# RWKV6 attention and an exact-GELU MLP on one core: six more zero products in the first tile

## The chip, the cores and the metric

The kernel runs on one core of a Trainium2 chip. The time is device microseconds of one execution; a kernel is timed several times and the median is given. An execution with the hardware profiler leaves the trace from which the times inside the kernel are read. They count from the start of the span, the time from the first instruction to the last.

## The reference

`r`, `k`, `v`, `w` have the shape (4, 8, 768, 48): 4 sequences, 8 heads, 768 steps, 48 channels. A linear attention with a decaying state runs over the steps, and its output goes through an MLP of 384 to 2048 to 384 with an exact GELU.

```python
for t in range(S):
    cur = np.einsum('bhd,bhe->bhde', u[None] * kt, vt)
    y[:, :, t] = np.einsum('bhd,bhde->bhe', rt, state + cur)
    state = wt[:, :, :, None] * state + np.einsum('bhd,bhe->bhde', kt, vt)
...
x = y.transpose(0, 2, 1, 3).reshape(B * S, H * D)
h = x @ w_in
g = 0.5 * h * (1.0 + erf(h * inv_sqrt2))
out = g @ w_out
```

## The kernel before, in words

**Tiles.** The 3072 tokens are cut into eight tiles of T = 384 steps, two for each sequence. `attention(x, unit)` is a Python generator that issues the attention of tile x, one step per `next()`; `mlp(x)` does the same for the MLP. While tile x's MLP runs, tile x + 1's attention is woven into it. The first tile has no MLP to be woven into. Its attention is cut into two units of four heads each, unit 0 and unit 1 (`units_of(0)` is 2, and 1 for every other tile), and these are woven into each other.

**The order by hand.** The scheduler is off. `PLAN[0]` is a string of letters that says which generator issues next: `.` is unit 0, `s` is unit 1, `l` is loads of weights and of tile 1's data, `c` is the conversion of weights, `f` is the attention of tile 1. Each engine executes its instructions in the order in which they were issued, and waits on semaphores for what it needs from the others. Unit 1 starts behind unit 0 and overtakes it at h = 16.

**Inside a unit.** Steps are taken in chunks of C = 64. For each unit there are NI = 6 pairs of chunks, and for each level h in 1, 2, 4, 8, 16, 32 three steps:

- `products` (L478 to L491): 24 products of 64 x 64 on TensorE, four for each of the six pairs of chunks (`g` and `p` each run over two halves of the partitions). An f32 product is executed as two passes, each with its own weight load (LDWEIGHTS) and product (MATMUL), so a call makes 48 pairs of instructions at line L485. For the levels from 2 to 16 it ends with `keep_warm(2)`, and the diagonal products of h = 1 do too.
- an update of `r` and `k` on VectorE (L563; L552 where they are updated one by one). It writes what the products have read, so it waits for them.
- a copy of the result out of PSUM into `a_sb`, with a mask on VectorE (L581) for h below 16, and by rows on ScalarE (L578) for h = 16. At h = 32 the copies are at L778.

After the levels, `k` is transposed on TensorE (L754, six products) and copied to SBUF on ScalarE (L767). Then come `kv` (L804: 24 products in f32, again 48 pairs of instructions), the products of the chunk matrices with `v` (L857), the chain over the states on VectorE (L836, L831), a copy of two columns as a fence (L867 or L870), the products of `r` with the states (L900), and the copy of the result into `xT` (L907, L923). In kv each index `i` of the six is four products of two passes, 8 pairs of instructions.

On TensorE, with u0 and u1 for the units, the order from the middle of the first tile on is: u0 h = 8, u1 h = 8, u1 h = 16, u0 h = 16, u1 h = 32, u1's transposes, u0 h = 32, u1's kv, u0's transposes, u1's L857, u0's kv, u1's L900, u0's L857, u0's L900. Then the first products of tile 1 (L501) and the first tile's MLP (L1299) follow.

**Zero products.** `keep_warm(n)` takes a bank of PSUM from the two with the tag "mm" and issues n products of a 128 x 128 matrix of zeros with 512 columns of zeros in bf16, each with its weight load. Nothing reads the result. Before the first products there is a `keep_warm(16)`. The tag "mm" is also used by the transposes of the first tile (`kt_ps`), by unit 0's `y_ps`, and by the MLP's banks.

**Instructions.** Each engine's instructions are read from memory by DMA while the kernel runs. In the trace, such transfers are of the kind "instruction", on queues 8 and 14.

Of the kernel before, what the change touches and what calls it, by code (L numbers as in the profile page):

```python
# [21 lines left out]
C = 64  # L22
# [6 lines left out]
NI = Q * N3  # L29
LEVELS = (1, 2, 4, 8, 16, 32)  # L30
# [46 lines left out]
def kernel(  # L77
# [47 lines left out]
    def pair(name):  # L125
        return pools["d"].tile([128, 2, BANK], F32, name=name, tag="d")
# [25 lines left out]
    def units_of(x):  # L152
        return NPART if x == 0 else 1
# [90 lines left out]
    def keep_warm(n):  # L244
        t = ps.tile([128, BANK], F32, name="warm", tag="mm", bufs=2)
        for _ in range(n):
            nc.tensor.matmul(t, lhsT=zeros[:, 0:128], rhs=zeros, start=True, stop=True)
# [42 lines left out]
    for i, h in enumerate(QUARTERS[:1]):  # L290
        for a in range(3):
            w_q = (3 - a) * C // 4
            z = q_ints[1 if a == 0 else 2]
# [82 lines left out]
    def attention(x, unit):  # L376
# [3 lines left out]
        np_ = len(parts)  # L380
# [6 lines left out]
        rc, kc = (z.rearrange("p (b i c t) -> p b i c t", b=np_, c=2, t=C) for z in (r, k))  # L387
# [87 lines left out]
        else:  # L475
            yield

        def products(bs, right, width, rest=False, last=False):  # L478
            d = pair("d")
            n = 0  # L480
            for b in bs:
                for i in range(NI):
                    for g in range(2):
                        for p in range(2):
                            nc.tensor.matmul(d[half[p], g, n * width:(n + 1) * width],  # L485
                                             lhsT=kc[half[g], b, i, p], rhs=right(half[g], b, i, p),
                                             start=True, stop=True)
                    n += 1
            if x == 0 and not rest and not last:
                keep_warm(2)  # L490
            return d[:, :, 0:n * width]  # L491

        def first_and_diagonal():

            width, each = 3 * C // 2, np_ * NI // 3
            for z in range(3):
                d = pair("d")
                for n in range(z * each, (z + 1) * each):
                    for g in range(2):
                        for p in range(2):  # L500
                            nc.tensor.matmul(d[half[p], g, (n - z * each) * width:(n - z * each + 1) * width],  # L501
                                             lhsT=kc[half[g], n // NI, n % NI, p], rhs=wide_r[half[g], 2 * n + p],
                                             start=True, stop=True)
                first_parts.append((at[:, :, z * each:(z + 1) * each],
                                    d[:, :, 0:each * width].rearrange("p g (n t) -> p g n t", t=width)))

        def copy_first_and_diagonal():
            for a, d in first_parts:
                a2 = a.rearrange("p g n (m two) -> p g n m two", two=2)[:, :, :, :, 1]
                for o, mask, data in ((a2, masks[1], d[:, :, :, 0:C // 2]), (a, masks[0], d[:, :, :, C // 2:])):  # L510
                    nc.vector.copy_predicated(out=o, mask=mask.unsqueeze(1).unsqueeze(1).to_broadcast(data.shape), data=data)
# [3 lines left out]
        def diagonal():  # L515
            return [products([b], lambda z, b, i, p: rucs[b][z, i, p], C) for b in range(np_)]

        def copy_diagonal(diag):
            for b in range(np_):
                nc.vector.copy_predicated(out=at[:, :, b * NI:(b + 1) * NI],  # L520
                                          mask=masks[0].unsqueeze(1).unsqueeze(1).to_broadcast([128, 2, NI, C]),
                                          data=diag[b].rearrange("p g (i t) -> p g i t", t=C))

        def halves():

            for h in LEVELS:
                m = C // 2 // h
                if x and h == 1:
                    first_and_diagonal()
                elif np_ < NPART:  # L530

                    d = products(range(np_), lambda z, b, i, p: rc[z, b, i, p], C, h == 1, h == LEVELS[-1])
                    d = d.rearrange("p g (n m two j) -> p g n m two j", two=2, j=h, m=m)[:, :, :, :, 1, :]
                else:
                    right = rc.rearrange("p b i c (m two j) -> p b i c m two j", two=2, j=h)[:, :, :, :, :, 1, :]
                    d = products(range(np_), lambda z, b, i, p: right[z, b, i, p], C // 2)
                    d = d.rearrange("p g (n m j) -> p g n m j", j=h, m=m)
                if h == 1:
                    yield
                    if x == 0:  # L540
                        diag = diagonal()
                yield

                r2 = r.rearrange("p (n two j) -> p n two j", two=2, j=h)[:, :, 1, :]
                t2 = tot[h].rearrange("p (n two) -> p n two", two=2)[:, :, 0:1].to_broadcast(r2.shape)
                k2 = k.rearrange("p (n two j) -> p n two j", two=2, j=h)[:, :, 0, :]
                tk = tot[h].rearrange("p (n two) -> p n two", two=2)[:, :, 1:2].to_broadcast(k2.shape)
                rk = bass.AP(tensor=r2.tensor, offset=r2.offset, ap=[r2.ap[0], [n_u - h, 2]] + list(r2.ap[1:]))
                tt = bass.AP(tensor=t2.tensor, offset=t2.offset, ap=[t2.ap[0], [1, 2]] + list(t2.ap[1:]))

                def update(z, r2=r2, t2=t2, k2=k2, tk=tk):
                    nc.vector.tensor_mul(*((k2, k2, tk) if z is k else (r2, r2, t2)))  # L552

                if x == 0 and m == 1:

                    update(k)
                    last_r.append(lambda: update(r))
                elif x == 0 and h == 1:
                    update(r)
                    yield  # L560
                    update(k)
                else:
                    nc.vector.tensor_mul(rk, rk, tt)  # L563
                yield
                if first_parts and h == 1:
                    copy_first_and_diagonal()
                    yield
                    continue
                ah = at.rearrange("p g n (m two j) -> p g n m two j", two=2, j=h)[:, :, :, :, 1, :]
                if x == 0 and m == 1:  # L570
                    last_rows.append((ah, d))
                    return
                if h >= 16:

                    for p in range(2):
                        for i in range(m):
                            s = slice(p * 64 + i * 2 * h, p * 64 + i * 2 * h + h)
                            nc.scalar.copy(out=ah[s, :, :, i], in_=d[s, :, :, i])  # L578
                else:
                    mask = masks[h].rearrange("p (m j) -> p m j", j=h).unsqueeze(1).unsqueeze(1)  # L580
                    nc.vector.copy_predicated(out=ah, mask=mask.to_broadcast(ah.shape), data=d)  # L581
                if h == 1:
                    copy_diagonal(diag)
                yield
# [154 lines left out]

        last_r, last_rows = [], []  # L740
        yield from halves() if x < 2 else quarters()


        if x < 2:
# [38 lines left out]
            def k_t(b, i, p, g):  # L783
                return kts[b][half[p], i, g, :]
# [9 lines left out]
        def vs(b, i, g):  # L794
            o = ((parts[b] * NI + i) * 2 + g) * D
            return loaded[x][1][:, o:o + G]

        kvs = []
        for b in range(np_):
            kv_ps = pair("kv_ps")  # L800
            for i in range(NI):
                for p in range(2):
                    for g in range(2):
                        nc.tensor.matmul(kv_ps[half[g], p, i * D:(i + 1) * D], lhsT=k_t(b, i, p, g),  # L804
                                         rhs=vs(b, i, g)[half[p], 0:D], start=True, stop=True)
            kvs.append(kv_ps[:, :, 0:NI * D].rearrange("p c (q i e) -> p q i c e", q=Q, e=D))
            if x > 0:
                o = parts[b] * Q * NC * D
                nc.scalar.copy(out=st[:, o:o + Q * NC * D].rearrange("p (i c e) -> p i c e", c=2, e=D),
                               in_=kv_ps[:, :, 0:NI * D].rearrange("p c (i e) -> p i c e", e=D))  # L810
# [628 lines left out]


    units = [attention(0, unit) for unit in range(units_of(0))]
    second = load_second(nc.sync)

# [104 lines left out]
```

## Time and profile before

| | us |
|---|---|
| median of 3 runs | 584.7 |
| lowest, highest | 584.18, 585.9 |
| the profiled execution | 587.26 |
| its span | 585.5 |
| TensorE busy in the first 6.17 us | 3.88 |
| TensorE busy from 6.17 to 46.18 us (40.01) | 29.83 |
| TensorE busy from 46.18 to 110 us (63.82) | 63.82 |
| TensorE's mean granted clock from 6.17 to 46.18 us | 0.91 |

The page gives for each engine the time in which at least one of its instructions was executing. PE is TensorE's products, PEld its weight loads, DVE is VectorE, ACT is ScalarE, and SP the engine that issues most of the DMAs. A view of instructions in order of time merges neighbours of one line and operation: start, length from the first start to the last end, how many (x), and in square brackets how long the engine sat idle before, and what ended that. "issue" means that the trace shows nothing that the engine waited for. Lengths of products hold a tail of about 0.2 us in which the result drains, and products that follow overlap it. Of each `keep_warm(2)` the trace has both weight loads and one of the two products. PEclk is the share of full speed that the clock gate granted to TensorE.

### The profile page before, as it was taken

How to read it: one execution, taken by the hardware profiler on the slowest of the kernel's cores; microseconds unless marked ns; L12 is line 12 of the kernel's file. 1: busy time of each engine (PE TensorE's matmuls, PEld its weight loads, DVE VectorE, ACT ScalarE, POOL GpSimd, SP SyncE). 2: the span in 40 equal slices, each digit the busy share in tenths (PEclk: the TensorE clock that was granted, in tenths of full speed). 3: DMA queues.
4: the chain of work that ended last, by engine and by line, in shares of the span. 5: the costliest groups of instructions: out<-in, count | busy, mean ns of one | idle time of the engine just before them, and what ended most of it. 6: DMA issues, size and time to landing. Idle time of an engine off the chain costs nothing. (4 is left out here: it accounts for less than half of the span.)

```text
span 585.5 us, 17244 instructions
## 1 busy us (share of the span) xinstructions
PE 569.1 (97%) x7407; PEld 507.7 (87%) x7418; DVE 460.2 (79%) x820; ACT 299.4 (51%) x735; POOL 8.0 (1%) x21
## 2 busy tenths in 40 slices
PE   7679999999999999999999999999999999999998
PEld 4466666766799999999999999999999999999997
DVE  7779877999768996698859998498759999884532
ACT  2565999432623556545554366455564366533400
POOL 4100000000000000000000000000000000000000
PEclk9989999999999999999999999999999999999999
DMA  7548771140222201441024201441013200210000
GB/s 248 188 154 295 253 260 55 34 142 3 41 75 78 75 3 31 124 135 57 2 55 122 74 21 19 115 139 38 2 32 116 68 2 1 43 40 7 1 15 34
DMA packets 51003, 46.79 MB, mean 80 GB/s; under 512 B 31728, under 2 KB 36080, under 8 KB 50928
## 3 DMA queue, kind: packets, MB, share of 16 engines
q1 hardware_dynamic: 50832, 45.62, 25.9%
q8 instruction: 58, 0.95, 0.7%
q14 instruction: 17, 0.14, 0.1%
q10 hardware_dynamic: 96, 0.07, 0.1%
HBM read 36.24 MB, written 4.72 MB: 70 GB/s over the span
## 5 line engine op out<-in xcount | busy, mean ns | idle before, releaser
L1087 PE MATMUL h_ps<-xT,w_in_sb 128*128 128x192 f32 x408 | 81.7, 331 | 0.4 <-DVE u L1429 0.3
L1087 PEld LDWEIGHTS h_ps<-xT,w_in_sb 128*128 128x128 f32 x408 | 67.6, 190 | 3.8 <-ACT g L1119 1.1
L1299 PE MATMUL h_ps<-xT,w_in_sb 128*128 128x384 f32 x192 | 64.2, 491 | 0.1
L1299 PEld LDWEIGHTS h_ps<-xT,w_in_sb 128*128 128x128 f32 x192 | 35.8, 190 | 23.9 <-ACT rkw L1407 0.2
L1313 PE MATMUL o_ps<-w_out_sb,g 128*128 128x192 f32 x224 | 39.5, 326 | 0.0
L1313 PEld LDWEIGHTS o_ps<-w_out_sb,g 128*128 128x128 f32 x224 | 36.9, 190 | 0.3
L669 ACT COPY a_sb<-d 32x256 f32<-32x256 f32 (+8 forms) x90 | 32.6, 362 | 3.3 <-PE d L653 1.4
L1313 PE MATMUL o_ps<-t,s 128*128 128x192 f32 x176 | 30.9, 328 | 0.0
L1313 PE MATMUL o_ps<-w_out_sb,f 128*128 128x192 f32 x176 | 30.9, 328 | 0.0
L1313 PE MATMUL o_ps<-t,g 128*128 128x192 f32 x176 | 30.8, 329 | 0.0
L1313 PE MATMUL o_ps<-t,e 128*128 128x192 f32 x176 | 30.7, 328 | 0.0
L1313 PE MATMUL o_ps<-w_out_sb,e 128*128 128x192 f32 x176 | 30.7, 328 | 0.0
L485 PEld LDWEIGHTS d<-rkw 64*64 64x64 f32 x1056 | 18.3, 140 | 13.6 <-issue 8.1
L1087 PE MATMUL u_ps<-s,w_in_sb 128*128 128x192 f32 x160 | 29.5, 328 | 0.0
L1313 PEld LDWEIGHTS o_ps<-t,s 128*128 128x128 f32 x176 | 28.8, 190 | 0.3 <-DVE u L1421 0.2
L1313 PEld LDWEIGHTS o_ps<-t,g 128*128 128x128 f32 x176 | 28.7, 190 | 0.3
L1313 PEld LDWEIGHTS o_ps<-w_out_sb,e 128*128 128x128 f32 x176 | 28.7, 190 | 0.2
L1313 PEld LDWEIGHTS o_ps<-w_out_sb,f 128*128 128x128 f32 x176 | 28.8, 190 | 0.2
L1313 PEld LDWEIGHTS o_ps<-t,e 128*128 128x128 f32 x176 | 28.7, 190 | 0.2
L1302 ACT ACTIVATE g<-h_ps 128x256 f32<-128x256 f32 (+1 forms) x32 | 13.8, 430 | 28.5 <-PE h_ps L1299 28.5
L485 PE MATMUL d<-rkw 64*64 64x64 f32 (+1 forms) x1056 | 20.9, 228 | 6.6 <-issue 4.2
L653 PE MATMUL d<-kx,rkw 64*64 64x96 f32 x1056 | 27.1, 247 | 0.0
(248 smaller groups left out, 1202.8 us busy)
## 6 DMA issues: line engine op xcount, KB each, us to landing
rkw<-in_rkw_dram SPq DMA_DIRECT2D x54, 256.0 KB, 3.6
raw<-in_w_out_dram SPq DMA_DIRECT2D x8, 768.0 KB, 4.8
v_in<-in_v_dram SPq DMA_DIRECT2D x8, 584.0 KB, 4.5
raw<-in_w_in_dram SPq DMA_DIRECT2D x5, 768.0 KB, 6.9
out_dram<-o_sb SPq DMA_DIRECT2D x20, 192.0 KB, 1.9
rkw<-kx SPq DMA_DIRECT2D x72, 48.0 KB, 2.0
rkw<-in_rkw_dram SPq DMA_DIRECT2D x6, 384.0 KB, 4.7
raw<-in_w_in_dram SPq DMA_DIRECT2D x9, 256.0 KB, 5.1
```

The source lines that it names most:

```text
L485: nc.tensor.matmul(d[half[p], g, n * width:(n + 1) * width], lhsT=kc[half[g], b, i, p], rhs=right(half[g], b, i, p), start=True, stop=True)
L653: nc.tensor.matmul(o[half[p], i * 3 * C // 2:(i + 1) * 3 * C // 2], lhsT=kc[half[g], n // NI, n % NI, p], rhs=rx[half[g], 2 * n + p], star ...
L669: nc.scalar.copy(out=at[z, g, first:behind, (a + 1) * h:], in_=d[z, :, :, to] if g == slice(None) else d[z, :, to])
L1087: nc.tensor.matmul(o, lhsT=lhsT, rhs=rhs, start=start, stop=True, skip_group_check=True)
L1299: nc.tensor.matmul(h_ps, lhsT=w_in_sb[:, f // FI, j, f % FI * 128:(f % FI + 1) * 128], rhs=xT[:, j, :], start=(j == 0), stop=(j == NJ - 1))
L1302: nc.scalar.activation(out=gs[group][:, f % FG, 0:t], in_=h_ps[:, 0:t], func=AF.Gelu)
L1313: nc.tensor.matmul(o, lhsT=lhs(j), rhs=rhs(j), start=start and j == 0, stop=(j == HF - 1), skip_group_check=True)
```

## The change

`products` gets an argument `hold`: after the `hold`-th pair of chunks, three zero products are issued inside the burst. It is set in one place, to 1, for unit 1 at h = 8. In kv, three zero products are issued after the fifth of the six indices, for unit 0 of the first tile alone. Nothing else differs.

```diff
-        def products(bs, right, width, rest=False, last=False):
+        def products(bs, right, width, rest=False, last=False, hold=None):
             d = pair("d")
             n = 0
             for b in bs:
...
                     n += 1
+                    if n == hold:
+                        keep_warm(3)
             if x == 0 and not rest and not last:
                 keep_warm(2)
...
-                    d = products(range(np_), lambda z, b, i, p: rc[z, b, i, p], C, h == 1, h == LEVELS[-1])
+                    d = products(range(np_), lambda z, b, i, p: rc[z, b, i, p], C, h == 1, h == LEVELS[-1], 1 if unit and h == 8 else None)
...
                         nc.tensor.matmul(kv_ps[half[g], p, i * D:(i + 1) * D], lhsT=k_t(b, i, p, g),
                                          rhs=vs(b, i, g)[half[p], 0:D], start=True, stop=True)
+                if units_of(x) > 1 and not unit and i == NI - 2:
+                    keep_warm(3)
             kvs.append(kv_ps[:, :, 0:NI * D].rearrange("p c (q i e) -> p q i c e", q=Q, e=D))
```

## The prediction

> **What bounds the kernel now.** I read the page first, then the engines' busy time in stretches of 3.41 us, then TensorE's instructions in order of time, then the DMA queues around its two longest waits.
>
> ```profile
> PE 569.1 (97%) x7407; PEld 507.7 (87%) x7418; DVE 460.2 (79%) x820; ACT 299.4 (51%) x735; POOL 8.0 (1%) x21
> ...
> q8 instruction: 58, 0.95, 0.7%
> ```
>
> TensorE is busy for 97% of the span, and the waits that the trace names for it lie almost all before 46 us. From there to the end its busy time has only about 1 us of holes, outside the last few microseconds. So what the first tile gains or loses by 44 us should reach the end nearly undiminished. Queue 8 carries 58 transfers of 0.95 MB, 16.4 KB each: instructions being fetched.
>
> ```profile
> core 0: us, PE busy (x) PEld busy (x) DVE busy (x) ACT busy (x) POOL busy (x), PEclk, DMA share, GB/s
> ...
> 16.41:19.82 3.41, 2.12 (x66) 1.35 (x68) 3.41 (x7) 3.38 (x6) 0.47 (x1) 1.00 0.81 210
> ...
> 23.24:26.65 3.41, 1.06 (x34) 0.71 (x35) 0.69 (x1) 0.62 (x1) 0.00 (x0) 1.00 0.35 114
> 26.65:30.06 3.41, 2.73 (x73) 2.14 (x78) 2.64 (x7) 3.38 (x6) 0.00 (x0) 0.50 0.21 72
> ...
> 36.89:40.30 3.41, 1.46 (x75) 1.34 (x65) 2.31 (x13) 2.48 (x3) 0.00 (x0) 1.00 0.29 107
> 40.30:43.72 3.42, 3.17 (x94) 2.98 (x93) 2.70 (x14) 0.48 (x1) 0.00 (x0) 0.50 0.07 16
> ```
>
> The granted clock (PEclk) is 0.50 in two stretches, each right behind a stretch in which TensorE was busy for 1.06 or 1.46 us of 3.41. Behind 2.12 us of 3.41 it stayed at 1.00. So the limit lies between 43% and 62% busy.
>
> ```profile
> start us, us, engine line op out<-in xcount [idle before <-releaser]
> ...
> 22.42 0.46 PE L485 MATMUL d<-rkw 64*64 64x64 f32 x15
> 25.19 0.73 PE L485 MATMUL d<-rkw 64*64 64x64 f32 x33 [2.31 <-issue]
> 25.85 0.39 PE L247 MATMUL warm<-zeros 128*128 128x512 bf16 x1
> 26.97 1.56 PE L485 MATMUL d<-rkw 64*64 64x64 f32 x48 [0.73 <-DVE rkw L563]
> 28.46 0.61 PE L247 MATMUL warm<-zeros 128*128 128x512 bf16 x1
> 29.43 1.20 PE L485 MATMUL d<-rkw 64*64 64x64 f32 x48 [0.36 <-issue]
> ...
> 39.53 0.26 PE L804 MATMUL kv_ps<-v_in,g 64*64 64x48 f32 x3 [1.95 <-issue]
> ...
> 41.28 1.54 PE L857 MATMUL y_ps<-a_sb,v_in 64*64 64x64 f32 x42
> 43.07 1.08 PE L900 MATMUL y_ps<-rkw,st 64*64 64x64 f32 x35 [0.25 <-DVE fence L867]
> ```
>
> The two idle times, 2.31 and 1.95 us, are put down to "issue", and both cut a run of like products in two: 15 + 33 of unit 1's h = 8 burst, and 43 + 5 of unit 0's kv. Between the two cuts I counted weight loads from 25.18 on, burst by burst: 33 + 2 + 48 + 2 + 48 + 2 + 48 + 6 + 48 + 48 + 6 + 48 + 43 = 382, each with a product, and four semaphore instructions (one at L485, one at L754, two at L804): 768, which is 3 x 256 to the instruction. 256 instructions in 16.4 KB is one transfer of queue 8. So TensorE waits at block ends for the next block. Its transfer starts near 22.79 and 37.08 us and takes about 1 us; work resumes about 1.4 us after it ends. Both start while data loads keep the DMA engines over 90% busy; with them idle the next fetch starts 1.15 us after a restart (25.19 to 26.34).
>
> The Trainium skill ("Runtime: NRT & Kernel Launch", Instruction fetch mechanics) gives the same blocks of 256, but calls the crossing "mostly hidden"; the rows show 2.31 us of it in the open.
>
> **The change, part by part.** Each site adds three zero products, so three weight loads and three products on TensorE; no DMA, nothing on other engines. Their tile takes a bank from the "mm" pair: at site 1 only earlier zero products used it, at site 2 ScalarE's copies of kt, which kv already awaits. I cost waits at nothing. Two extra turns leave the pair's order for y as it was.
>
> *Price of three.* The pair at 14.98 us lets the next burst start at 15.52, 0.54 us for two; at half clock, 28.46 to 29.43, 0.97 us. Three by proportion: 0.81 us, and 1.46 at half clock. Least, if only the products' own streaming counts, about 0.6.
>
> *Site 1* (unit 1, h = 8, after `n == 1`): one matrix is 4 matmuls of two passes, so 8 pairs, 16 instructions. The block end lies 30 instructions into this burst; now it holds 16 + 6 + 8. The products run before the wait; idle shrinks from 2.31 to about 1.5 us. The fetch at 22.79 was asked for when the block began and doesn't depend on them, so the restart stays at 25.19. Three pairs of real work move behind it: 33 pairs took 0.73 us less 0.22 of tail, so 3 x 0.016 = **+0.05 us**. If the cover were gone it would cost 0.81. For the clock: the stretch from 23.24 gains some 0.2 us of work, 1.06 to about 1.25 of 3.41, still under 43%. The stretches may fall elsewhere in another execution, but the two idle times (1.5 and 0.7 us) lie close together, so mostly the clock still drops.
>
> *Site 2* (unit 0's kv, after `i == NI - 2`): 5 matrices are 40 pairs, 80 instructions. The old block end stood at 43 pairs, 86 instructions. But site 1's six instructions, three blocks earlier, move it six forward: to exactly 80. **The three products then are the first of the new block.** They don't fill the wait; they stand behind it, ahead of the last 8 pairs of kv, of both y steps (L900, L857) and of VectorE's chain. Idle stays near 1.95 us and the stretch behind it still runs at 0.50.
>
> Their path, with the stretches as profiled: restart 39.53 + 0.81 = 40.34, where the half clock begins. What was done from 39.53 to 42.82 is 0.77 us at full clock and 2.52 at half, 2.03 in full-speed time. To 43.72 only 3.38 / 2 = 1.69 fits; the rest, 0.34, ends at 44.06. Fence 0.25, then unit 0's L900, 43.07 to 44.10, which is 0.65 at half and 0.38 at full, 0.71: 45.02 against 44.10, **+0.92 us**. Were the clock full throughout it would be 0.81, and with only the streaming 0.6; with the products at half clock, 1.46. I take 0.85, between the two likely cases.
>
> *Sum:* 0.05 + 0.85 = **+0.9 us**. The profiled execution took 587.26 us, 585.5 of it span; the sum would make its span 586.4. It is 2.6 us above the median of the runs, so I carry the difference over: 584.7 + 0.9 = **585.6 us**. A measurement can tell about 0.3% (1.75 us) from no change, so this is "within".
>
> A rule that speaks against any gain from the clock stands in the Trainium skill ("TensorE: Matmul & The Clock Gate", Part 1, What's actually happening): the clock halves only after an idle window of about 3.4 us. By that rule neither wait would cost clock, the sum would be +0.86, and the gains of B, C and E below would be nought. The trace differs: 0.50 behind waits of 2.31 and 1.95 us.
>
> **The rivals.** *B, the first half-clock stretch is avoided:* then unit 1's h = 16 burst takes about 0.93 us instead of 1.56.
>
> ```profile
> 30.33 2.56 ACT L578 COPY a_sb<-d 16x192 f32<-16x192 f32 x8
> 33.35 0.86 ACT L767 COPY g<-kt_ps 128x384 f32<-128x384 f32 x2 [0.46 <-PE kt_ps L754]
> ```
>
> ScalarE is full until 32.89 with or without it, and its kt copies gate kv, so only their 0.46 us of waiting can go: 585.6 - 0.5 = 585.1; at most 1.2, what TensorE's own queue would gain. For: idle falls to 1.5 us. Against: 0.7 more follow at once.
>
> *C, site 2 does run ahead of its block end* (my count is off by more than a few instructions): idle falls to about 1.1 us, the stretch holds 2.3 us of work, above the 62% that kept the clock. Then the DVE chain ends at 42.04, the fence at 42.3, and the last pairs of L900 wait for the block fetched from 40.63 (42.97): L501 begins near 43.35, not 44.10. -0.75 + 0.05: 584.0. Against it stands 768.
>
> *E, both:* 583.5, and 582.8 with B's upper gain.
>
> *D, slower:* the fetch asked for at the block end near 30.2 us (it starts at 31.66, takes 1.47) is late. It has no slack: 33.14 + 1.4 is when unit 1's kv crosses the next end, 34.6. If its request, now moved by six instructions, falls behind the loads that fill the DMA engines from 31 us, it may start up to 2.6 us later (the worst fetch took 4.07 us from block start, 18.72 to 22.79; this one 1.46). Half of that, 1.3, falls on kv: +2.2 in all, 586.9. It decides once the request comes behind those loads. Against: six instructions are only 0.05 us.
>
> **How the numbers follow.** Forecast 0.52, B 0.15, C 0.13, E 0.04, D 0.16. The forecast's own range is 584.9 to 586.4 (0.6 to 1.46 for site 2, and the spread of the runs). The range 583.7 to 587.0 holds it, B, most of C and half of D. Faster by over 0.3% (under 582.95): 0.06, from E and C's tail. Slower (over 586.45): 0.17, most of D and the forecast's edge. Within: 0.77.
>
> **What would show it.** Right: 8 pairs of L485, three zero products, 4 pairs, then a wait ending near 25.2; exactly 40 pairs of L804, the wait of about 1.9 us, and the zero products first behind it; PEclk 0.50 after both. Wrong: zero products ahead of the second wait, PEclk at 1.00 from 40 to 44, or a new wait near 34 us.

## The result, and the profile after

| | before | with the change |
|---|---|---|
| median, us (22 runs each) | 585.12 | 586.16 |
| lowest to highest | 583.69 to 586.37 | 584.91 to 587.95 |
| ratio of the times | | 1.0018, 95% interval 1.0010 to 1.0026 |
| span of the profiled execution | 585.5 | 584.4 |

The change makes the kernel 1.04 us slower (by the interval 0.6 to 1.5 us); 0.9 us was forecast. The profiled execution is a shorter one than that of before. A kernel's executions differ among themselves by 2 to 3 us, so two spans can't be set against each other for a difference of this size; the profiles are read for the order of events, and the times are taken from the medians.

This is the new kernel's TensorE in order of time (start, length, engine, line, operation, tile, shapes, count, and what ended the idle time before):

```profile
23.02 0.34 PE L485 MATMUL d<-rkw 64*64 64x64 f32 x8
23.30 0.82 PE L247 MATMUL warm<-zeros 128*128 128x512 bf16 x3
24.05 0.33 PE L485 MATMUL d<-rkw 64*64 64x64 f32 x4
24.69 0.80 PE L485 MATMUL d<-rkw 64*64 64x64 f32 x36 [0.31 <-issue]
...
33.70 0.94 PE L806 MATMUL kv_ps<-v_in,g 64*64 64x48 f32 x48 [0.88 <-ACT g L769]
...
36.14 0.75 PE L806 MATMUL kv_ps<-v_in,g 64*64 64x48 f32 x40
38.43 0.82 PE L247 MATMUL warm<-zeros 128*128 128x512 bf16 x2 [1.55 <-issue]
39.19 0.33 PE L806 MATMUL kv_ps<-v_in,g 64*64 64x48 f32 x8
39.34 1.17 PE L904 MATMUL y_ps<-rkw,st 64*64 64x64 f32 x34
```

The first trio stands in its burst as 8, three, 4, then the wait, then 36. In unit 0's kv (now L806) exactly 40 pairs run, then TensorE waits 1.55 us for the next block of instructions, and only then come the zero products and the last 8 pairs. (Of the second trio the trace has all three weight loads and two of the products.) From the restart to the first product of kv is 39.19 - 38.43 = 0.76 us.

The clock, in the same stretches of 3.41 us as before, laid on the new profile's own grid (the last three figures of a row are PEclk, the DMA share and GB/s):

```profile
17.09:20.50 3.41, 1.89 (x66) 1.35 (x70) 3.41 (x7) 3.24 (x5) 0.69 (x1) 1.00 0.72 181
...
34.15:37.57 3.42, 2.74 (x127) 2.39 (x118) 2.96 (x14) 3.11 (x6) 0.00 (x0) 1.00 0.62 236
37.57:40.98 3.41, 2.49 (x86) 2.01 (x91) 1.36 (x8) 1.46 (x3) 0.00 (x0) 1.00 0.02 5
40.98:44.39 3.41, 2.89 (x152) 2.76 (x145) 3.35 (x12) 1.07 (x3) 0.00 (x0) 1.00 0.19 46
```

In this execution the granted clock stayed at 1.00 until its last microsecond (the mean from 580 us to the end is 0.92). The grid lies otherwise: the wait, 36.89 to 38.43, is shared by two stretches, and TensorE was busy for 2.74 and 2.49 us of them, more than the 2.12 us that kept the clock before. So the trio costs its time here at full clock too, with no help from a half-clock stretch.

### The profile page after: what moved, and what is told of

Same layout as the page of the kernel before. It is cut to its first block, busy times and chain, and to the rows that moved or that the text cites. A ratio compares the mean times of both kernels' runs of the same rounds, so it can differ in the third digit from the quotient of the medians.

```text
span 584.4 us, 17255 instructions
## 1 busy us (share of the span) xinstructions
PE 569.3 (97%) x7412; PEld 506.2 (87%) x7424; DVE 459.5 (79%) x820; ACT 299.9 (51%) x735; POOL 8.0 (1%) x21
## 5 line engine op out<-in xcount | busy, mean ns | idle before, releaser
L401 DVE TRANSPOSE_TENSOR_REDUCE rkw<-kx 128x48 f32<-128x1536 f32 (+3 forms) x24 | 27.0, 1154 | 0.1
```

What stands on the lines that cost most here:

```text
L401: nc.vector.tensor_reduce(out=fine_sb[:, e, 0:n].rearrange("p a n -> p (a n)"), in_=kx[:, o:o + n * n_m].rearrange("p (m j) -> p m j", j=3 ...
```

## The experiments

All against the kernel before, on the same chip as it and interleaved with it. "Second site" is the one in kv. Where an edit is shown as a diff it is against the changed kernel.

**The first trio alone.**

```diff
-                if units_of(x) > 1 and not unit and i == NI - 2:
+                if False:
                     keep_warm(3)
```

> Only the three products in unit 1's h = 8 burst. Theory (block ends): they run before the first long wait and are hidden in it; the long wait in unit 0's kv stays, now behind exactly 40 pairs of L804. Expected against the kernel before: -0.3 to +0.2 us (three pairs moved behind the restart cost 0.05, a half-clock stretch less often gains up to 0.5). Rival (each trio costs TensorE its own time wherever it stands, about half of the measured +1.0 us): +0.5 us.

Measured: 584.81 against 584.95 us, ratio 0.9997 (0.9988 to 1.0006). The first trio costs nothing that can be measured (-0.7 to +0.4 us), and the rival's +0.5 us lies outside the interval. Its profile, TensorE in order of time:

```profile
23.15 0.82 PE L247 MATMUL warm<-zeros 128*128 128x512 bf16 x3
23.90 0.33 PE L485 MATMUL d<-rkw 64*64 64x64 f32 x4
24.81 0.80 PE L485 MATMUL d<-rkw 64*64 64x64 f32 x36 [0.58 <-issue]
...
37.96 0.33 PE L806 MATMUL kv_ps<-v_in,g 64*64 64x48 f32 x8 [1.58 <-issue]
38.12 1.17 PE L904 MATMUL y_ps<-rkw,st 64*64 64x64 f32 x34
```

The block end stands 8 pairs before the end of kv, as with the change: the six instructions moved it there. From the restart to L904 it is 0.16 us here and 0.91 with the change, 0.75 more; from the restart to the MLP's first product 5.71 (37.96 to 43.67) and 6.36 (38.43 to 44.79), 0.65 more.

**The second trio alone.** `hold` stays at None everywhere.

> Only the three products in unit 0's kv. Theory (block ends): without the first three the block end stays at 86 instructions into kv, and 40 pairs and the three products fill it exactly, so the products run before the wait and it shrinks from 1.95 to about 1.2 us with the restart unmoved; the half-clock stretch behind it goes. Expected: -0.7 to 0.0 us. Rival (own time wherever it stands): +0.5 us or, if the second site alone is the cost, +1.0.

Measured: 584.63 against 584.95 us, ratio 0.9996 (0.9986 to 1.0006). The same three products in the same place of the program, and the cost is gone (-0.8 to +0.4 us). TensorE in order of time:

```profile
35.35 0.75 PE L806 MATMUL kv_ps<-v_in,g 64*64 64x48 f32 x40
36.03 0.82 PE L247 MATMUL warm<-zeros 128*128 128x512 bf16 x2
38.18 0.33 PE L806 MATMUL kv_ps<-v_in,g 64*64 64x48 f32 x8 [1.33 <-issue]
```

Without the first trio the block ends six instructions later, and 40 pairs and the trio fill it to the last one. The trio runs, then comes the wait. This is the reading that the whole case rests on: the rows are the same as with the change, in another order.

**Both trios, the second one pair of chunks earlier.**

```diff
-                if units_of(x) > 1 and not unit and i == NI - 2:
+                if units_of(x) > 1 and not unit and i == NI - 3:
```

> Both trios, but the second one pair of chunks earlier in kv (after the fourth of six), which puts it 64 instructions into kv and so ahead of the block end at 80. Theory (block ends): both waits shrink, no trio is on the path: -0.9 to 0.0 us. Rival (own time wherever): +1.0 us as with the change, since the same products are executed.

Measured: 584.76 against 584.95 us, ratio 1.0000 (0.9990 to 1.0010). As many zero products as with the change, no cost (-0.6 to +0.6 us). TensorE in order of time:

```profile
36.09 0.63 PE L806 MATMUL kv_ps<-v_in,g 64*64 64x48 f32 x32
36.66 0.82 PE L247 MATMUL warm<-zeros 128*128 128x512 bf16 x2
37.41 0.32 PE L806 MATMUL kv_ps<-v_in,g 64*64 64x48 f32 x5
38.58 0.37 PE L806 MATMUL kv_ps<-v_in,g 64*64 64x48 f32 x10 [0.85 <-issue]
...
42.58 0.39 PE L904 MATMUL y_ps<-rkw,st 64*64 64x64 f32 x10 [0.42 <-issue]
```

32 pairs, three zero products, 5 pairs: 64 + 6 + 10 = 80 instructions, where the count put the block end. The last row is a wait at the next block end, which this profile also has.

**Both trios, the first with hardly any work.** Six instructions remain, with 16 columns instead of 512.

```diff
-    def keep_warm(n):
+    def keep_warm(n, cols=BANK):
...
-            nc.tensor.matmul(t, lhsT=zeros[:, 0:128], rhs=zeros, start=True, stop=True)
+            nc.tensor.matmul(t[:, 0:cols], lhsT=zeros[:, 0:128], rhs=zeros[:, 0:cols], start=True, stop=True)
...
-                        keep_warm(3)
+                        keep_warm(3, 16)
```

> As the change, but the first three zero products have 16 columns instead of 512: nearly no work, the same six instructions. Theory (block ends): the six instructions still push the block end ahead of the second trio, so the cost stays: +0.7 to +1.2 us. Rival (own time wherever): the first trio's share is gone, +0.5 us.

Measured: 585.99 against 584.95 us, ratio 1.0016 (1.0001 to 1.0031). The interval, 0.1 to 1.8 us, holds the rival's +0.5 too, so the time alone doesn't decide. The rows do: the first trio takes 0.23 us instead of 0.82, and the second trio is again behind the wait. It isn't the first trio's work that puts it there; its instructions do:

```profile
22.72 0.23 PE L247 MATMUL warm<-zeros 128*128 128x16 bf16 x3
...
35.90 0.75 PE L806 MATMUL kv_ps<-v_in,g 64*64 64x48 f32 x40
37.88 0.82 PE L247 MATMUL warm<-zeros 128*128 128x512 bf16 x2 [1.23 <-issue]
```

**Both trios, six old instructions left out between them.** `products` gets a count for the zero products behind its burst: none for unit 1 at h = 8, one at h = 16.

```diff
-            if x == 0 and not rest and not last:
-                keep_warm(2)
+            if x == 0 and not rest and not last and warm:
+                keep_warm(warm)
...
-..., 1 if unit and h == 8 else None)
+..., 1 if unit and h == 8 else None, {8: 0, 16: 1}.get(h, 2) if unit else 2)
```

> Both trios where the change has them, and three of the old zero products behind unit 1's bursts left out (both at h = 8, one at h = 16), six instructions, so that the block end in kv is back at 86 and the second trio fits ahead of it. Theory (block ends): the change's cost goes: -0.7 to +0.1 us. Rival (the second trio costs where it stands in kv, whatever the blocks): +1.0 us, or +0.8 without the one product that lay on TensorE's path.

Measured: 585.28 against 585.25 us, ratio 1.0002 (0.9987 to 1.0017). Both sites stand where the change has them, and no cost is seen. The interval, -0.8 to +1.0 us, is wide and just holds the rival's numbers; what the rows show is that the block ends behind the second trio again:

```profile
35.71 0.75 PE L806 MATMUL kv_ps<-v_in,g 64*64 64x48 f32 x40
36.39 0.82 PE L247 MATMUL warm<-zeros 128*128 128x512 bf16 x2
37.80 0.33 PE L806 MATMUL kv_ps<-v_in,g 64*64 64x48 f32 x8 [0.59 <-issue]
```

**One trio only, at the end of kv.** `hold` at None, and `i == NI - 1`.

> No first trio; the second one after the sixth pair of chunks of kv instead of the fifth, 96 instructions in and so behind the block end, which is back at 86. The same three products as in the run with the second site alone, 8 pairs later. Theory (block ends): they are on the path again: +0.5 to +1.1 us over the kernel before. Rival (one trio alone costs nothing, it takes both): 0.0 us.

Measured: 586.24 against 585.25 us, ratio 1.0021 (1.0005 to 1.0037). One trio alone costs about what the change costs when it lies behind the block end (0.3 to 2.2 us); it doesn't take both. In its profile 43 pairs run, the wait is 1.98 us, 5 pairs follow, then the trio:

```profile
34.67 0.85 PE L806 MATMUL kv_ps<-v_in,g 64*64 64x48 f32 x43
37.50 0.32 PE L806 MATMUL kv_ps<-v_in,g 64*64 64x48 f32 x5 [1.98 <-issue]
37.76 0.82 PE L247 MATMUL warm<-zeros 128*128 128x512 bf16 x2
```

**Six at the second site instead of three.** The first trio as with the change.

```diff
                 if units_of(x) > 1 and not unit and i == NI - 2:
-                    keep_warm(3)
+                    keep_warm(6)
```

> As the change, with six zero products at the second site instead of three. Theory (block ends): they all stand behind the block end, each of the three more costs its streaming time, about 0.22 us, on the path: +0.65 us over the change, +1.4 to +1.9 us over the kernel before. Rival (the cost is the block end's new place or the clock, not the products behind it): +1.0 us as with the change.

Measured: 588.69 against 585.25 us, ratio 1.0054 (1.0037 to 1.0072): 3.2 us, clearly more than the change, so products behind the block end do add up. But it is 1.3 us more than the upper end of what was expected, and its profile shows something new ahead of the MLP:

```profile
37.60 1.47 PE L247 MATMUL warm<-zeros 128*128 128x512 bf16 x5 [1.49 <-issue]
39.00 0.33 PE L806 MATMUL kv_ps<-v_in,g 64*64 64x48 f32 x8
...
45.68 1.56 PE L1303 MATMUL h_ps<-xT,w_in_sb 128*128 128x384 f32 x4 [1.06 <-ACT xT L911]
48.41 8.01 PE L1303 MATMUL h_ps<-xT,w_in_sb 128*128 128x384 f32 x24 [1.17 <-DMA xT<-ysb]
```

The six take 1.40 us up to kv, 0.64 more than three. Beside that this execution has 2.2 us of waits for `xT` (1.06 + 1.17): ScalarE issues three small DMAs at L943, and the last of them took 2.23 us here, against 0.6 to 0.9 in the other profiles; its copy at L911 is behind that in ScalarE's queue, and the transfer landed late. Seven of its 11 executions took over 588.5 us, as the profiled one did, so whatever adds to the time was in most of them. Two runs were made for this.

**Six at the end of kv, no first trio.**

> No first trio; six zero products after the sixth pair of chunks of kv, all behind the block end. The run with six at the change's place came out at +3.2 us instead of the expected +1.4 to +1.9, and its profile shows the last of ScalarE's three xT transfers being issued 1.6 us slower than elsewhere, with TensorE waiting for xT ahead of the MLP. If six products cost only their streaming time: +1.3 to +1.9 us over the kernel before, and no wait for xT. If the delay in the xT transfers comes with six products (a collision of the later xT transfers with the next block's fetch): +2.5 to +3.5 us and that wait again.

Measured: 586.99 against 585.50 us, ratio 1.0027 (1.0011 to 1.0044), 1.6 us (0.6 to 2.6). That fits the products' own time, 1.40 us in its rows, as first expected, though the interval reaches into the other range. Its profile has 0.9 us of waiting for xT from landed transfers, with the issues at 0.6 to 0.9 us each, so a short form of the wait was there, though the time had been expected to come without it.

**The six once more, for a second profile.**

> The run with six products at the change's second site once more, for a second profile. If the slow issue of the xT transfer belongs to this timing, it is there again (over 1.5 us for one, where the others take 0.6 to 0.9) with TensorE waiting about 2 us ahead of the MLP; if it was chance, the issue takes under 1 us and the MLP's first product follows the first products of tile 1 at once.

Measured: 587.35 us, one execution, on another chip than the first run with six. The issues take 0.61 to 0.86 us, and the MLP follows at once:

```profile
38.53 1.47 PE L247 MATMUL warm<-zeros 128*128 128x512 bf16 x6 [1.71 <-issue]
39.93 0.33 PE L806 MATMUL kv_ps<-v_in,g 64*64 64x48 f32 x8
...
45.48 10.20 PE L1303 MATMUL h_ps<-xT,w_in_sb 128*128 128x384 f32 x30
```

So the six products don't always bring the slow issue. Whether they bring it more often, and whether it explains the 3.2 us, two profiles can't tell, and it stays open.

**One zero product instead of two behind each burst, neither trio.** An attempt at a better kernel: 20 instructions fewer ahead of kv move the block end out of it.

```diff
             if x == 0 and not rest and not last:
-                keep_warm(2)
+                keep_warm(1)
```

> Neither trio, and one zero product instead of two behind each burst of the first tile: 20 instructions fewer ahead of kv, so the block end leaves kv and falls 10 instructions into unit 1's L900. All of kv then runs before the wait and VectorE's chain over unit 0's states (about 2.1 us) runs during it. Theory (block ends): the fence wait of 0.5 us and the last 8 pairs leave the path: -0.4 to -1.1 us. Rival (fewer zero products let the clock drop more often): +0.3 to +1.5 us.

Measured: 585.44 against 585.25 us, ratio 1.0005 (0.9990 to 1.0021). The block end went where the count put it, 5 pairs into unit 1's L904, and the wait for VectorE's fence is 0.26 us, against 0.52 with the change (0.25 in the profile before, whose products ran at half clock there). But the next block then has to be waited for as well, 0.43 us within the first products of tile 1:

```profile
36.56 0.39 PE L904 MATMUL y_ps<-rkw,st 64*64 64x64 f32 x5
37.20 1.09 PE L904 MATMUL y_ps<-rkw,st 64*64 64x64 f32 x30 [0.24 <-issue]
...
39.42 0.80 PE L904 MATMUL y_ps<-rkw,st 64*64 64x64 f32 x35 [0.26 <-DVE fence L871]
...
40.93 2.19 PE L503 MATMUL d<-kx,rkw 64*64 64x96 f32 x91 [0.43 <-issue]
```

No gain and no loss could be told: the interval, -0.6 to +1.2 us, holds the weak end of both. The rival's mechanism did come, though not in the profiled execution: by the mean clock on record for each execution (how to read it stands below), 9 of 12 had a half-clock stretch, against 11 of 34 of the kernel before. The three without one weren't shorter either, 585.05 us on average against 585.08. No kernel was found that beats the one before by more than its interval.

## Why the prediction was right

**The sum.** +0.9 us was forecast and 1.04 measured (0.6 to 1.5). The time, 586.16 us, lay within the range and within the 0.3% of "no change". Of the 0.56 us between it and the 585.6 of the forecast, 0.42 is the kernel before, which measured 585.12 us over 22 runs and not 584.7.

**The count to 256** held to the instruction: 40 pairs with the change, 40 and the trio with the second site alone, 32 + 3 + 5 with the second site moved, 43 without the first trio. This is shown, not only argued: each trio alone at its place costs nothing that can be measured, and the two together cost 1.0 us, in rows that have the second trio ahead of the wait or behind it as the count says. Six instructions with next to no work, some 15 us earlier, put it behind (+0.9 us, 0.1 to 1.8), and six old ones left out put it ahead again (0.0 us, -0.8 to +1.0).

**Site 1 at +0.05:** the first trio alone measured -0.2 us (-0.7 to +0.4), so too small to see. That its time is hidden in the wait is seen in the rows. The restart was forecast at 25.2 and came at 24.69, and the wait was 0.31 us instead of about 1.5. Its fetch began at 22.34 us and not at 22.79, while this execution's burst started 0.6 us later. So it began 3.0 us after the block's first product (19.32), against 4.07 us before; that the data loads of the moment set this is likely, but no run tested it. The 1.4 us from the fetch's end to the restart held (23.27 to 24.69); at the block end in or just behind kv it was 1.2 to 1.6 us over the twelve profiles.

**Site 2 at +0.85:** the wait stands where it was forecast, at 1.55 us instead of about 1.95. The trio was priced at 0.81 from the pair at 14.98; it took 0.76 up to the next product, and 0.65 of that reached the MLP in the two profiles compared above. The path that gave +0.92 assumed a half-clock stretch behind the wait. The profiled execution had none, so that this part of the working was right in its result but not as it was told. That it did no harm is luck: the path at full clock, 0.81, and the one with the half-clock stretch, 0.92, happen to cost nearly the same. The one at full clock is the better account.

**The half clock** was the forecast's weakest part. It was expected after both waits, and PEclk at 1.00 from 40 to 44 us was named as a sign of being wrong; in the profiled execution that sign came. Over all profiles the half clock comes and goes. Before has it twice, the narrow first trio once (26.23 to 29.64), the trio at the end of kv once (38.94 to 42.35), the second look at six once, and the other eight not before their last microsecond. The limit read from the profile before, between 43% and 62% busy, is too sharp a picture: 1.89 us of 3.41 kept the clock with the change, 1.95 lost it in the second look at six. So the busy share alone doesn't set it.

```profile
17.11:20.52 3.41, 1.95 (x56) 1.17 (x58) 2.72 (x5) 3.38 (x7) 0.00 (x0) 1.00 0.80 259
20.52:23.93 3.41, 3.41 (x90) 2.46 (x94) 2.38 (x7) 0.31 (x2) 0.00 (x0) 0.50 0.89 301
```

The Trainium skill's rule ("TensorE: Matmul & The Clock Gate", Part 1, What's actually happening), half clock only after an idle window of 3.4 us, isn't what these rows show: 1.95 us of work in the window, and half clock in the next. But its other statement, that the window is free-running, fits that the grid starts at 6.17 us in one profile and at 6.85 in another.

The mean granted clock that each execution has on record tells how often this came. In the profiles it is 0.994 with two half-clock stretches, 0.997 with one, and 0.999 or 1.000 with none before the last microsecond. Read so, and with 0.996 taken as one, 10 of the 22 executions of the change had one or two stretches, and 12 had none. These 12 took 586.0 us on average; the executions of the kernel before without a stretch, in the three series of experiments, took 584.7 to 585.1. So the cost of the change isn't one of the clock.

**The rivals.** B (first half-clock stretch avoided, -0.5): no such stretch came in the profiled execution, and kv then waited 0.88 us for ScalarE's copy, which is the cap that B was given. But the first trio alone measured -0.2 us, with an interval that holds both nought and B's 0.5. The clocks on record say more. With the first trio alone, the second alone, or the second one pair of chunks earlier, where no trio lies behind a block end, 2 of 34 executions had a half-clock stretch; of the kernel before, beside them, 11 of 35 had one. So zero products that run into a wait keep the clock up more often here. It is worth little: of these 35, the executions with a stretch took 1.0 us longer on average than those without, and a quarter fewer of them is about 0.3 us, an estimate, which is less than the intervals can show. C (the second trio runs ahead of the block end) is what the second trio does alone, and there it was worth -0.2 us (-0.8 to +0.4), mostly short of the -0.7 that C was given, which the interval just holds: shortening a wait whose end the fetch sets brought nothing that could be measured. E needs both sites ahead of their block ends, as in the run with the second one earlier: 0.0 us (-0.6 to +0.6), not the -1.2 that E was given. D (a late fetch, a new wait near 34 us) isn't there: the profile has a new wait near 34 us, a sign that was named, but it is the one ahead of kv at 33.70, for ScalarE's copy and not for a block.

## What to carry to other kernels

Where the engine that bounds the time waits for its next block of instructions, work put ahead of the block end is free as long as the wait covers it, and work behind it is not, and a few instructions decide which it is. So count instructions from one such wait to the next, and count again after each edit: instructions added at one place move every later block end, and may undo an edit that was placed by the old profile. And filling a wait shortens the idle time in the profile, but hardly the time, as long as what ends the wait doesn't come earlier.

## What the runs showed that was not expected

- The wait at the same block end varies much between executions: ahead of the last 33 pairs of unit 1's h = 8, with no zero products in the burst, it was 2.31 us before, 0.94 with the second trio alone and 0.67 with the trio at the end of kv.
- A DMA issue on ScalarE's queue, 0.6 to 0.9 us in eleven profiles, took 2.23 us in one, and TensorE waited 2.2 us for xT ahead of the MLP.
- With fewer instructions ahead, the wait for one block came out shorter (0.24 us), and a wait for the next one appeared (0.43 us); so it did with the second trio one pair of chunks earlier (0.42 us). From restart to restart these two took 3.7 us (37.20 to 40.93) and 4.0 us (38.58 to 42.58): in this stage the pace of the fetches is a limit of its own.
